# Scores of the first eight attention units: 64 contracted rows against 128 rows with zeros in the queries

## The chip, the cores and the metric

The kernel runs on one core of a Trainium2 chip. The core has five engines with a queue of instructions each: PE (TensorE, matrix products; its weight loads are shown apart as PEld), DVE (VectorE), ACT (ScalarE), POOL (GpSimd) and SP (SyncE, which here only issues DMAs). The metric is the device time of one execution in microseconds (us), lower is better.

## What is computed

Forgetting attention over 4 batches, 8 heads, 576 positions and 64 dimensions, then two MLPs of 512 -> 2048 -> 512 on the 2304 rows, all in float32:

```python
scores = scale * np.matmul(q, k.transpose(0, 1, 3, 2))
cum = np.cumsum(np.maximum(s, 0.0), axis=-1)
bias = -(cum[:, :, :, None] - cum[:, :, None, :])
scores = np.where(causal, -1e9, scores + np.minimum(bias, 0.0))
attn = softmax(scores)            # sum + 1e-09 below
x = matmul(attn, v), heads side by side
x = (s * relu(x @ w_in) ** 2 + b) @ w_out
h = x @ w_in2;  out = (max(h, 0) + alpha * min(h, 0)) @ w_out2
```

## The kernel before

Attention is cut into 32 units: one batch, one pair of heads, and either the first 320 queries (blocks 0, 1, 2) or the last 256 (blocks 3, 4), with all keys up to the last query. A unit's pair of heads lies on the 128 partitions, head 0 on rows 0 to 63 and head 1 on rows 64 to 127.

For each unit `load_qk` brings q and k to a tile `nat`; `transpose_qk` turns both on DVE (L308, in 32x32 blocks) into `turned`, so that the 64 dimensions of each head lie on its half of the partitions; `scores` (L320 on) prepares the bias (DVE L362, POOL L366), multiplies, folds the product into the bias on DVE (L388) and takes the exponential on ACT (L394), and POOL divides by the sum (L403); `values` transposes the probabilities on PE (L434), copies them out of PSUM (L438) and multiplies with v (L450, tile `av`).

Units 0 to 7 are "native": their products are plain float32. For them the scores' product (L384) takes only the head's own half, 64 rows of `turned` as the stationary and 64 as the moving operand. From unit 8 on q and k are split into high and low parts (`xs`, `ql`; L326 to L332), and L386 and L387 multiply on all 128 rows. The eight native units have 48 products at L384; in the trace each is two instructions, so 96 are counted there. Units 1 to 3 are also "early": their buffers are slots of the weight memory that is still empty. Units 4 to 7 hold 256 queries each and 576 keys, the units 0 to 3 320 and 320.

Beside attention runs the first MLP: `load_packet` brings 512 KB pieces of weights, and ACT (L116), DVE (L117, L118), ACT and POOL (L106, L107) turn them into two float32r parts. Row block 0 of the MLP (products L575 and L616) begins when units 0 to 3 are done, and shares the engines with units 4 to 7 and with the conversion of the weights. ACT and DVE form its inner activations (L596, L598, L599), ACT and POOL split them (`gh`, `gl`).

A scheduler orders the instructions of every engine before the launch, by priority in program order and by a timeline of its own; each engine then runs its queue in that fixed order. Tiles with the same tag share memory: a new tile waits for the last reader of the one before it. `turned` has one buffer (tag `turned`) for the units 0 and 4 to 31, so a unit's transposes wait for the last scores product of the unit before. The tiles `ql` are zeroed on the other head's half once, at the start, on POOL (L204).

Of the kernel before, what the change touches and what calls it, by code (L numbers as in the profile page):

```python
# [8 lines left out]
F32 = mybir.dt.float32  # L9
F32R = mybir.dt.float32r  # L10
# [8 lines left out]
def tile_forget_attention__then__two_mlps(  # L19
# [20 lines left out]
    nc = tc.nc  # L40
# [3 lines left out]
    P = 128  # L44
# [7 lines left out]
    R1 = IB[2][1]  # L52
    QK = S - R1 + S
# [12 lines left out]
    one = ctx.enter_context(tc.tile_pool(name="one", bufs=1))  # L66
# [131 lines left out]

    ql_tiles = [[one.tile([P, R1], F32R, tag=f"ql{h}{n}", name=f"ql{h}{n}") for n in range(1 + h)] for h in range(2)]
    for h in range(2):
        for t in ql_tiles[h]:
            nc.gpsimd.memset(t[64 * (1 - h) : 64 * (2 - h)].bitcast(F32), 0.0)  # L204
    vs_tile = one.tile([P, 5 * 4 * D], F32R, tag="vs", name="vs_all")
    nc.gpsimd.memset(vs_tile[0:64, 16 * D :].bitcast(F32), 0.0)

# [3 lines left out]
    HALF = (slice(0, 64), slice(64, 128))  # L211
# [36 lines left out]
    def qk_tiles(u, dtype, tag):  # L248

        nq, nk = u.q1 - u.q0, u.q1  # L250
        if u.early:
            q_tile, k_tile = (u.buf(one, 512, dtype, "", f"{tag}{z}") for z in "qk")
            return [q_tile[:, :nq], k_tile[:, :nk]], q_tile[:, :nq], k_tile[:, :nk]
        both = one.tile([P, QK], dtype, tag=tag, name=f"{tag}_{u.tag}")
        return [both[:, : nq + nk]], both[:, :nq], both[:, nq : nq + nk]

    def load_qk(u):

        u.nats, *parts = qk_tiles(u, F32, "nat")
        for src, dst, t0, t1 in ((q, parts[0], u.q0, u.q1), (k, parts[1], 0, u.q1)):  # L260
            for h in range(2):
                for e in range(2):
                    (nc.scalar if u.n == 0 and src is k else nc.sync).dma_start(  # L263
                        out=dst[64 * h + 32 * e : 64 * h + 32 * (e + 1)].rearrange("p (c d) -> p c d", d=32),
                        in_=src[u.b, u.h0 + h, t0:t1, 32 * e : 32 * (e + 1)].rearrange("(c p) d -> p c d", p=32),
                    )
# [35 lines left out]
    def transpose_qk(u):  # L302


        nq = u.q1 - u.q0
        turned, *u.qk = qk_tiles(u, F32, "turned")
        for dst, src in zip(turned, u.nats):
            nc.vector.transpose(dst, src)  # L308
        yield
        if u.native:  # L310
            return
        if u.n >= 12 and u.n % 2:

            xs = [two.tile([P, 1024], F32R, tag="raw", name=f"xs{h}_{u.tag}") for h in range(2)]
        else:
            xs = [one.tile([P, QK], F32R, tag=f"xs{h}", name=f"xs{h}_{u.tag}") for h in range(2)]
        u.ql = [ql_tiles[h][u.n % len(ql_tiles[h])] for h in range(2)]
        u.xs = [[x[:, :nq], x[:, nq : nq + u.q1]] for x in xs]
        for h in range(2):
            own, other = HALF[h], HALF[1 - h]  # L320
            (qh, kh), (qt, kt) = u.xs[h], u.qk
            if u.early:
                nc.scalar.copy(qh[own], qt[own])
                nc.scalar.copy(kh[own], kt[own])
            else:
                nc.scalar.copy(xs[h][own, : nq + u.q1], turned[0][own])  # L326
            nc.gpsimd.tensor_scalar(
                out=qh[other], in0=qt[own], scalar1=1.0, scalar2=0.0, op0=ALU.mult, op1=ALU.add
            )
            yield  # L330
            nc.vector.tensor_tensor(out=kh[other], in0=kt[own], in1=kh[own].bitcast(F32), op=ALU.subtract)  # L331
            nc.vector.tensor_tensor(  # L332
                out=u.ql[h][own, :nq], in0=qt[own], in1=qh[own].bitcast(F32), op=ALU.subtract
            )
            yield

    def scores(u, h):

        own = HALF[h]
        head = u.b * H + u.h0 + h  # L340
        nr = len(u.blocks)
        nm = two.tile([P, 3], F32, tag="nm", name=f"nm_{u.tag}_{h}")
        sm = two.tile([P, 3], F32, tag="sm", name=f"sm_{u.tag}_{h}")
        if u.rng == 0:
            nc.gpsimd.memset(sm[:, 0:1], 1.0)
        big = None if u.early else two.tile([P, 1088], F32, tag="probs", name=f"probs_{u.tag}_{h}")
        probs, col = {}, 0
        for r in u.blocks:
            i0, i1 = IB[r]
            rows = i1 - i0  # L350
            if u.early and r != 1:
                big, col = u.buf(two, 0, F32, "", f"probs{h}{r}"), 0

            width = -(-i1 // P) * P if i1 < S else S
            pt = probs[r] = big[:, col : col + width]
            col += width
            if width > i1:
                nc.gpsimd.memset(pt[:, i1:], 0.0)  # L358
            if r == 0:
                nc.gpsimd.memset(pt[64:P, 0:64], 0.0)  # L360

            nc.vector.tensor_scalar(  # L362
                out=pt[:rows, :i1], in0=u.cums[h][:rows, :i1], scalar1=cumT[:rows, r, head : head + 1],
                scalar2=0.0, op0=ALU.subtract, op1=ALU.min,
            )
            nc.gpsimd.affine_select(  # L366
                out=pt[:rows, i0:i1], in_=pt[:rows, i0:i1], pattern=[[-1, rows]], base=0,
                channel_multiplier=1, compare_op=ALU.is_ge,
                fill=MASKED,
            )  # L370
        u.probs[h] = probs
        for m, r in enumerate(u.blocks):
            i0, i1 = IB[r]
            rows, n = i1 - i0, i1
            a0 = i0 - u.q0
            pt = probs[r]
            init = KEEP_ALL
            for j0, j1 in ([(0, n)] if n <= 512 else [(0, 320), (320, n)]):
                sc = u.bank("sc", f"sc{h}_{r}_{j0}")

                scr, all_ = sc[:rows, : j1 - j0], sc[:, : j1 - j0]
                aq = slice(a0, a0 + P)
                if u.native:
                    nc.tensor.matmul(all_, u.qk[0][own, aq], u.qk[1][own, j0:j1], start=True, stop=True)  # L384
                else:
                    nc.tensor.matmul(all_, u.xs[h][0][:, aq], u.xs[h][1][:, j0:j1], start=True, stop=False)  # L386
                    nc.tensor.matmul(all_, u.ql[h][:, aq], u.xs[h][1][:, j0:j1], start=False, stop=True)  # L387
                nc.vector.tensor_tensor_reduce(  # L388
                    out=pt[:rows, j0:j1], in0=scr, in1=pt[:rows, j0:j1], scale=-SCALE, scalar=init,
                    op0=ALU.add, op1=ALU.min,  # L390
                    accum_out=nm[:rows, m : m + 1],
                )
                init = nm[:rows, m : m + 1]
            nc.scalar.activation(  # L394
                pt[:rows, :n], pt[:rows, :n], AF.Exp, bias=nm[:rows, m : m + 1], scale=-1.0,
                accum_out=sm[:rows, m : m + 1],
            )
            yield
        nc.vector.tensor_scalar(out=sm[:, :nr], in0=sm[:, :nr], scalar1=1e-9, scalar2=None, op0=ALU.add)
        nc.vector.reciprocal(sm[:, :nr], sm[:, :nr])  # L400
        for m, r in enumerate(u.blocks):
            rows, n = IB[r][1] - IB[r][0], IB[r][1]
            nc.gpsimd.tensor_scalar(  # L403
                out=probs[r][:rows, :n], in0=probs[r][:rows, :n], scalar1=sm[:rows, m : m + 1],
                scalar2=1.0, op0=ALU.mult, op1=ALU.mult,
            )
        yield
# [73 lines left out]
    def attention():  # L481
        nonlocal done
        us = [Unit(n) for n in range(EARLY)]
        load_qk(us[0])
        sum_gates()
        load_cum(us[0])
        load_qk(us[1])
        load_v(us[0])
        load_cum(us[1])
        packet(0, 0)  # L490
        load_qk(us[2])
        load_cum(us[2])
        load_v(us[1])
# [7 lines left out]
        for u in us:  # L501
            split_v(u)
        yield from transpose_qk(us[0])
        yield from alternate(transpose_qk(us[1]), scores(us[0], 0))
        yield from alternate(transpose_qk(us[2]), scores(us[0], 1))
        yield from alternate(transpose_qk(us[3]), scores(us[1], 0), values(us[0], 0))
        yield from alternate(scores(us[1], 1), values(us[0], 1))
        yield from alternate(scores(us[2], 0), values(us[1], 0))
# [226 lines left out]
```

## Time and profile before

| | us |
|---|---|
| median of three runs | 1091.94 (1088.45, 1091.94, 1092.47) |
| the profiled execution | 1088.58 |
| its span, first to last instruction | 1086.8 |
| PE busy | 1045.6 (96%) |
| DVE, ACT, POOL busy | 666.8, 644.4, 478.4 |
| mean granted clock of PE | 0.985 of full speed |

Rows of a table of stretches give: from and to (us from the span's start), length, busy time and number of instructions of each engine, the mean granted clock of PE as a share of full speed (1.00 is 2.4 GHz, 0.50 is 1.2 GHz), the mean busy share of the DMA engines, and GB/s. Rows of a timeline give the start, the time until the end of the last of the instructions put together, engine, line, operation, output and inputs, shape, count, and in brackets the idle time of the engine before them with what ended it. Ends of products are modelled; the distance from one start to the next is the better measure of what a product takes.

### The profile page before, as it was taken

Reading aid. Unit: us, or ns where it says so; the run is one execution under the profiler, and the core shown is the slowest. Engines: PE = TensorE matmul, PEld = TensorE weight load, DVE = VectorE, ACT = ScalarE, POOL = GpSimd, SP = SyncE. Lnnn points to the kernel's source line nnn. Section 1 sums busy time; section 2 is a strip of 40 time slices with the busy share of each in tenths; the row PEclk is TensorE's granted clock in tenths of the full one; section 3 lists DMA queues with packets and bytes.
Section 4 is the critical chain, followed back from the end, with each engine's and each line's share of the span. In section 5 each row is a group of like instructions: output and inputs, shape, how many; then the busy total and the mean of one; then the engine's idle time right before and its main releaser. Section 6 shows DMA issues by size and latency. Waiting matters only on the chain.

```text
span 1086.8 us, 21253 instructions
## 1 busy us (share of the span) xinstructions
PE 1045.6 (96%) x7429; PEld 969.9 (89%) x7429; DVE 666.8 (61%) x1612; ACT 644.4 (59%) x1719; POOL 478.4 (44%) x868
## 2 busy tenths in 40 slices
PE   5899999999999999999999999899999999999998
PEld 3677799999999999999998999789999999999997
DVE  7699878787688877787565167943333333333332
ACT  3686767777767877777565467643444434434332
POOL 6688877665766757666464267820000000000000
PEclk9699899999999999999999999999999999999999
DMA  6987433343232422233134064510100100000000
GB/s 145 236 234 221 136 70 81 80 99 56 50 81 65 109 50 60 67 78 81 34 104 141 12 204 155 175 40 1 40 20 20 40 1 20 2 20 20 2 20 20
DMA packets 170059, 83.85 MB, mean 77 GB/s; under 512 B 135456, under 2 KB 155936, under 8 KB 169952
## 3 DMA queue, kind: packets, MB, share of 16 engines
q1 hardware_dynamic: 168272, 81.94, 28.3%
q8 instruction: 58, 0.95, 0.4%
q10 hardware_dynamic: 1680, 0.57, 0.2%
q14 instruction: 49, 0.40, 0.1%
HBM read 72.96 MB, written 9.51 MB: 76 GB/s over the span
## 4 chain that ended last, share of the span: by engine, by line
PE 67%; DVE 14%; DMA 5%; issue 4%; ACT 4%; POOL 3%; SPq 2%; DVEq 0%; POOLq 0%; ACTq 0%
PE hp L575 29%; PE acc L626 18%; PE acc L616 12%; PE pt L434 3%; DVE probs L362 3%; PE av L450 3%; DMA wo<-in_moe_w_out_dram 2%; DVE probs L388 2%; DVE wt L117 2%; DVE wt L118 2%; SPq L263 1%; DVE r L599 1%; DVE xs L331 1%; PE sc L387 1%; PE sc L386 1%
## 5 line engine op out<-in xcount | busy, mean ns | idle before, releaser
L575 PE MATMUL hp<-xh,w 128*128 128x256 f32 x2304 | 467.5, 285 | 5.6 <-ACT r L596 2.9
L575 PEld LDWEIGHTS hp<-xh,w 128*128 128x128 f32 x2304 | 378.6, 191 | 13.5 <-ACT r L596 4.4
L575 PE MATMUL hp<-xl,w 128*128 128x256 f32 x1152 | 327.2, 284 | 0.0
L575 PEld LDWEIGHTS hp<-xl,w 128*128 128x128 f32 x1152 | 220.3, 191 | 6.3 <-POOL probs L358 0.7
L626 PE MATMUL acc<-w,ring 128*128 128x512 f32 x864 | 220.4, 393 | 1.2 <-POOL ring L107 0.8
L616 PE MATMUL acc<-gh,w 128*128 128x256 f32 x1024 | 201.9, 288 | 5.3 <-ACT gh L106 5.0
L604 DVE SCALAR_TENSOR_TENSOR ring<-ring,nalpha 128x256 f32<-128x256 f32 x144 | 74.6, 520 | 177.3 <-ACT ring L603 176.3
L626 PEld LDWEIGHTS acc<-w,ring 128*128 128x128 f32 x864 | 154.1, 189 | 28.1 <-POOL ring L107 1.2
L616 PEld LDWEIGHTS acc<-gh,w 128*128 128x128 f32 x1024 | 161.1, 191 | 10.7 <-ACT gh L106 7.4
L616 PE MATMUL acc<-gl,w 128*128 128x256 f32 x512 | 149.4, 292 | 2.8 <-POOL gl L107 2.7
L596 ACT ACTIVATE ring<-hp 128x256 f32<-128x256 f32 x144 | 55.5, 385 | 138.6 <-PE hp L575 138.4
L107 POOL TENSOR_TENSOR gl<-r,gh 128x256 fp32r<-128x256 f32 x128 | 99.9, 781 | 63.8 <-ACT gh L106 62.6
L403 POOL TENSOR_SCALAR probs<-probs,sm 64x64 f32<-64x64 f32 (+4 forms) x160 | 93.5, 597 | 61.0 <-DVE sm L400 57.9
L394 ACT ACTIVATE probs<-probs,nm 64x64 f32<-64x64 f32 (+4 forms) x160 | 90.0, 562 | 46.3 <-DVE nm L388 44.9
L599 DVE TENSOR_SCALAR r<-r,gate_s,gate_b 128x256 f32<-128x256 f32 x144 | 80.5, 559 | 58.0 <-ACT r L598 55.8
L106 ACT CAST ring<-ring 128x256 fp32r<-128x256 f32 x144 | 58.5, 407 | 77.3 <-DVE ring L604 65.7
L616 PEld LDWEIGHTS acc<-gl,w 128*128 128x128 f32 x512 | 97.7, 191 | 5.2 <-POOL gl L107 5.1
L107 POOL TENSOR_TENSOR w<-wt,w 128x512 fp32r<-128x512 f32 x63 | 90.4, 1441 | 26.2 <-ACT w L106 22.1
L107 DVE TENSOR_TENSOR ring<-ring,ring 128x256 fp32r<-128x256 f32 x128 | 54.4, 425 | 61.1 <-ACT ring L106 61.1
L434 PE MATMUL pt<-ident,probs 128*128 128x128 f32 x480 | 79.8, 285 | 8.4 <-POOL probs L403 7.8
L388 DVE CUSTOM_DVE_ANT_0 probs<-sc,probs 128x320 f32<-128x320 f32 (+3 forms) x160 | 67.9, 427 | 23.9 <-PE sc L387 18.4
L596 ACT ACTIVATE r<-hp 128x256 f32<-128x256 f32 x144 | 54.6, 379 | 39.3 <-PE hp L575 33.2
(86 smaller groups left out, 1637.2 us busy)
## 6 DMA issues: line engine op xcount, KB each, us to landing
wi<-in_moe_w_in_dram SPq DMA_DIRECT2D x32, 512.0 KB, 4.5
wo<-in_moe_w_out_dram SPq DMA_DIRECT2D x32, 512.0 KB, 5.0
cum<-cum_d SPq DMA_DIRECT2D x32, 288.0 KB, 3.5
cum<-cum_d SPq DMA_DIRECT2D x30, 160.0 KB, 3.1
nat<-in_k_dram SPq DMA_DIRECT2D x64, 72.0 KB, 2.3
x_d<-res SPq DMA_DIRECT2D x18, 256.0 KB, 2.4
x<-x_d SPq DMA_DIRECT2D x9, 512.0 KB, 4.3
out_dram<-res SPq DMA_DIRECT2D x18, 256.0 KB, 2.0
```

Of the source, the lines that this page charges most:

```text
L106: nc.scalar.copy(hi, src)
L107: lo_eng.tensor_tensor(out=lo, in0=src, in1=hi.bitcast(F32), op=ALU.subtract)
L388: nc.vector.tensor_tensor_reduce(out=pt[:rows, j0:j1], in0=scr, in1=pt[:rows, j0:j1], scale=-SCALE, scalar=init, op0=ALU.add, op1=ALU.min, ...
L394: nc.scalar.activation(pt[:rows, :n], pt[:rows, :n], AF.Exp, bias=nm[:rows, m : m + 1], scale=-1.0, accum_out=sm[:rows, m : m + 1],)
L403: nc.gpsimd.tensor_scalar(out=probs[r][:rows, :n], in0=probs[r][:rows, :n], scalar1=sm[:rows, m : m + 1], scalar2=1.0, op0=ALU.mult, op1=A ...
L434: nc.tensor.transpose(tp[:, o : o + P], u.probs[h][r][:, k0 : k0 + P], ident)
L575: nc.tensor.matmul(hs, a[:, c], b[:, c], start=(n == 0), stop=(n == len(terms) * NCC - 1))
L596: nc.scalar.activation(r, hs, AF.Relu, scale=1.0 / W_SCALE)
L599: nc.vector.tensor_scalar(out=r, in0=r, scalar1=gate_s[:, 0:1], scalar2=gate_b[:, 0:1], op0=ALU.mult, op1=ALU.add)
L604: nc.vector.scalar_tensor_tensor(out=r, in0=u, scalar=nalpha[:, f : f + 1], in1=r, op0=ALU.mult, op1=ALU.add)
L616: nc.tensor.matmul(acc[:, d], a[:, d * P : (d + 1) * P], b, start=(f == 0 and d % 2 == 0 and n == 0), stop=(f == NF - 1), skip_group_check ...
L626: nc.tensor.matmul(accs[:, m * DM : (m + 1) * DM], a[:, m * P : (m + 1) * P], b, start=(f == 0 and b is woh and a is gh), stop=(f == NF - ...
```

## The change

The queries of the native units go into one of three pairs of zeroed tiles, `qz`, taken in turn (unit number modulo 3). Tile h of a pair holds the queries of head h on its own half and zeros on the other half, so that the product over all 128 rows of queries and keys is the score of that one head. The keys of both heads stay together in one tile.

- The pairs lie in memory that is unused until unit 8: two in the tags `xs0` and `xs1`, the third in the tags `ql00` and `ql10`. The first pair is zeroed on DVE, the other two on POOL, at the start.
- The three tiles `ql` are now made and zeroed (POOL) in the first call of `transpose_qk` for a unit that isn't native, unit 8.
- For a native unit DVE makes three transposes in place of one (unit 0, units 4 to 7) or two (units 1 to 3): the keys on 128 partitions, then the queries of each head on 64 partitions.
- L384 multiplies `qz[h]` with the keys on all 128 rows.
- The early units take one slot of weight memory less each.

```diff
-    ql_tiles = [[one.tile([P, R1], F32R, tag=f"ql{h}{n}", name=f"ql{h}{n}") for n in range(1 + h)] for h in range(2)]
-    for h in range(2):
-        for t in ql_tiles[h]:
-            nc.gpsimd.memset(t[64 * (1 - h) : 64 * (2 - h)].bitcast(F32), 0.0)
+    def zeroed(h, tile_, eng):
+        eng.memset(tile_[64 * (1 - h) : 64 * (2 - h)].bitcast(F32), 0.0)
+        return tile_
+
+    qz = []
+    for n in range(3):
+        if n < 2:
+            both = one.tile([P, QK], F32, tag=f"xs{n}", name=f"qz{n}")
+            pair = [both[:, :R1], both[:, R1 : 2 * R1]]
+        else:
+            pair = [one.tile([P, R1], F32, tag=f"ql{h}0", name=f"qz{n}{h}") for h in range(2)]
+        qz.append([zeroed(h, t, nc.gpsimd if n else nc.vector) for h, t in enumerate(pair)])
+    ql_tiles = []
...
         u.nats, *parts = qk_tiles(u, F32, "nat")
+        u.nat = parts
...
         nq = u.q1 - u.q0
+        if u.native:
+            kt = u.buf(one, 512 if u.early else QK, F32, "turned", "turnedk")[:, : u.q1]
+            nc.vector.transpose(kt, u.nat[1])
+            u.qk = [q_[:, :nq] for q_ in qz[u.n % 3]], kt
+            for h in range(2):
+                nc.vector.transpose(u.qk[0][h][HALF[h]], u.nat[0][HALF[h]])
+            yield
+            return
         turned, *u.qk = qk_tiles(u, F32, "turned")
         for dst, src in zip(turned, u.nats):
             nc.vector.transpose(dst, src)
         yield
-        if u.native:
-            return
+        if not ql_tiles:
+            for h in range(2):
+                tiles = [one.tile([P, R1], F32R, tag=f"ql{h}{n}", name=f"ql{h}{n}") for n in range(1 + h)]
+                ql_tiles.append([zeroed(h, t, nc.gpsimd) for t in tiles])
...
-                    nc.tensor.matmul(all_, u.qk[0][own, aq], u.qk[1][own, j0:j1], start=True, stop=True)
+                    nc.tensor.matmul(all_, u.qk[0][h][:, aq], u.qk[1][:, j0:j1], start=True, stop=True)
```

## Rows read from the trace of the kernel before

**Rows 1.** The page, span in 40 slices: granted clock of PE in tenths.
```profile
PEclk9699899999999999999999999999999999999999
```

**Rows 2.** Stretches: PE, PEld, DVE, ACT, POOL busy (count), PEclk, DMA share, GB/s.
```profile
28.00:47.00 19.00, 18.60 (x64) 12.49 (x62) 9.48 (x45) 12.24 (x39) 10.25 (x26) 0.55 0.86 206
57.00:85.00 28.00, 27.82 (x166) 22.42 (x164) 26.41 (x51) 21.23 (x50) 23.51 (x26) 0.94 0.90 255
85.00:111.00 26.00, 21.88 (x126) 17.77 (x124) 25.40 (x48) 18.32 (x42) 21.22 (x23) 0.93 0.77 215
111.00:134.00 23.00, 22.80 (x126) 18.81 (x127) 20.41 (x37) 16.61 (x41) 20.09 (x23) 0.85 0.49 134
165.00:560.00 395.00, 388.19 (x3181) 381.69 (x3180) 306.00 (x842) 289.00 (x776) 257.84 (x539) 1.00 0.31 70
```

**Rows 3.** Stretches at half clock; the last row: PE and PEld of L384 alone.
```profile
30.00:47.00 17.00, 16.60 (x52) 11.26 (x51) 8.61 (x41) 11.21 (x34) 8.53 (x20) 0.50 0.86 212
88.00:91.30 3.30, 3.30 (x16) 3.19 (x16) 3.30 (x6) 2.11 (x6) 1.72 (x3) 0.50 0.46 81
112.00:118.50 6.50, 6.50 (x25) 5.21 (x25) 6.50 (x15) 5.01 (x13) 4.58 (x6) 0.50 0.51 117
...
30.00:47.00 17.00, 5.93 (x16) 2.85 (x15) 0.50 0.86 212
```

**Rows 4.** Timeline of PE around three runs of products.
```profile
36.89 2.07 PE L384 MATMUL sc<-turnedk,turnedq 64*128 64x192 f32 x6
38.90 0.69 PE L434 MATMUL pt<-ident,probs 128*128 128x128 f32 x2
...
75.32 1.95 PE L450 MATMUL av<-pf,vn 128*128 128x256 f32 x10
77.08 0.36 PE L575 MATMUL hp<-xh,w 128*128 128x256 f32 x1
...
80.02 0.27 PE L434 MATMUL pt<-ident,probs 128*128 128x128 f32 x1
80.22 1.23 PE L384 MATMUL sc<-turned 64*128 64x320 f32 x4
81.39 0.51 PE L616 MATMUL acc<-gh,w 128*128 128x256 f32 x2
81.73 1.04 PE L434 MATMUL pt<-ident,probs 128*128 128x128 f32 x8
82.53 0.36 PE L575 MATMUL hp<-xh,w 128*128 128x256 f32 x1
```

**Rows 5.** Timeline of PE: the longest idle times before instructions, 85 to 145 us.
```profile
87.11 1.07 PE L384 MATMUL sc<-turned 64*128 64x448 f32 x2 [0.68 <-DVE turned L308]
111.19 0.51 PE L616 MATMUL acc<-gh,w 128*128 128x256 f32 x2 [1.88 <-ACT gh L106]
141.48 0.33 PE L434 MATMUL pt<-ident,probs 128*128 128x128 f32 x1 [0.43 <-POOL probs L403]
```

**Rows 6.** Chain that ended last, in order of time: start, us, what.
```profile
31.11 0.45 PE pt L434
...
36.96 0.95 PE sc L384 x3
...
38.31 0.66 SPq L263
```

**Rows 7.** The transposes: all of L308 (ns min/median/max, first and last start), and timeline of DVE.
```profile
L308 DVE STREAM_TRANSPOSE turned<-nat x29: 823/1023/1037, 6.0 to 509.3; 128x832 f32<-128x832 f32 x16, 128x640 f32<-128x640 f32 x13
L308 DVE STREAM_TRANSPOSE turnedq<-natq x3: 471/492/497, 11.0 to 26.0; 128x320 f32<-128x320 f32 x3
...
86.02 1.03 DVE L308 STREAM_TRANSPOSE turned<-nat 128x832 f32<-128x832 f32 x1
86.98 0.44 DVE L388 CUSTOM_DVE_ANT_0 probs<-sc,probs,nm 128x256 f32<-128x256 f32 x1
```

**Rows 8.** The zeroing of the tiles ql, all of L204.
```profile
L204 POOL MEMSET ql<- x3: 358/358/364, 1.0 to 1.7; 64x320 f32 x3
```

## The prediction

> **What bounds the kernel now.** I read the slices first, then tables of stretches, then PE's timeline where the change lies. The slices show where the clock of PE falls: only in the first 135 us [rows 1]. The stretches show who is full. From 165 us on PE is busy 388 of 395 us at full clock [rows 2]; the later stages are alike, so what is won or lost before that point reaches the end one for one, and nothing behind it touches the change. All of L384 lies before 134 us. There three stages differ. From 28 to 47 us PE is busy 18.6 of 19 us while DVE, ACT and POOL are about half idle, and PE's clock is 0.55 [rows 2]: PE at half speed (1.2 GHz) is the bound, with DMA (0.86) close behind. From 85 to 111 us DVE is busy 25.4 of 26 us and PE 21.9 [rows 2]: DVE, full of weight conversions, is the bound. From 57 to 85 us both are nearly full. From 111 to 134 us PE is busy 22.8 of 23 us, DVE 20.4: PE again, part of it at half clock [rows 2, 3].
>
> **Part A, 64 rows become 128.** The products keep their columns. What goes is what surrounds them. The run of v products takes 1.76 us from its start to the next start, for 256, 256, 256, 192 and 64 columns: 1.72 ns a column [rows 4]. A burst of scores of 320 + 256 columns would take 0.99 us at that rate; it takes 1.17 (80.22 to 81.39), and the one transpose record before it takes 0.20 from start to start where eight take 0.80, or 0.10 each [rows 4]. So 0.18 + 0.10 = 0.28 us a burst belong to the passage into and out of 64 rows. Units 4 to 7 have four bursts each; 13 start between 57 and 134 us. Four start after 111 us (111.7, 121.9, 125.7, 131.8), where PE has no gap: 4 x 0.28 = 1.1 us, counted in full. The other nine (2.5 us) lie where DVE is full or nearly so and PE already waits for it, as at 87.11 [rows 2, 5]: I count 0 of them (bounds 0 and 2.5).
>
> **Part B, the clock.** PE fell to half clock at about 30, 57, 88 and 112 us, each time after it had stood idle; the idle time of 1.88 us at 111.19 is one [rows 2, 3, 5]. What differs is how long it stayed low. From 57 us, with one burst of scores at the start, it was back after 3.4 us (0.94 of 28 us), and from 88 us, with a single record of 64-row scores left, after 3.4 too. From 112 us, with a burst of scores behind the fall, it stayed 6.9 us, and from 30 us, where 5.9 of 16.6 busy us are 64-row scores, 17 us, though PE was never long idle [rows 3]. No row shows what 128-row scores would do; the ends are no change and no fall at all. I take the length of the rows with few scores, 3.4 us, for all.
> From 112 us this brings back 3.4 us at half clock, worth 1.7 us, on a stretch that PE bounds (bounds 0 and 3.4).
> From 30 us, the chain of waits tells how much of the time passes on: it goes through PE from 31.11 to 37.91 us and then to the loads on SP at 38.31 [rows 6]. With full clock from 33.4 us, the 4.5 us of PE work left to 37.91 take half: 2.2 us. Ends: only the passages of two bursts, 0.6, and all 6.8 us at full clock, 3.4. DMA is busy 0.86 of 19 us [rows 2], so more than 2.7 us could not pass on without a better use of DMA, which is why I don't go beyond the middle.
>
> **Part C, the transposes on DVE.** Units 4 to 7 had one of 832 columns, 1.03 us, 0.96 from start to start; one of 320 takes 0.49 [rows 7]. Between them a column costs about 1.05 ns, so 576 columns take 0.76 and 256 take 0.43: three make 1.62, and with 0.07 of overlap at each of two more joints the queue grows by 0.45 us. If half the partitions cost half (no row shows a 64-partition transpose), it would be 0.02; without overlap 0.59. I take 0.45, since shapes that differ in columns alone are the nearest rows. The transposes of units 5, 6 and 7 fall into the full stretch (86.02 is one): 3 x 0.45 = 1.4 us on DVE's path (bounds 0.1 and 1.8). For units 0 to 4 the gain of 0.4 to 0.5 us each is covered by DVE's idle half before 47 us; without that cover, 2.2 us more. Against that, the queries go to three pairs in turn and need not wait for the scores of the unit before; only the keys do (0.76 instead of 1.03). I count nothing for it.
>
> **Part D, zeroing.** At the start two memsets go to DVE and one more than before to POOL, some 0.36 us each [rows 8], well before the first transposes at 6.0 us [rows 7]: nothing. The three of `ql` move to unit 8, about 134 us, in POOL's queue ahead of the casts for `xs` and the divisions for PE's transposes: 3 x 0.36 = 1.1 us. PE waits for POOL there once, 0.43 us at 141.48 [rows 5]; I take 0.4 (bounds 0 and 1.1). The waits of unit 8's `xs` for `qz` end no later than its own transposes, which wait for the same scores. One slot less for each early unit shifts which weights wait for which buffer; those weights are converted long after the early units: nothing.
>
> **Sum**, against the profiled execution of 1088.58: -1.1 (A) - 1.7 - 2.2 (B) + 1.4 (C) + 0.4 (D) = -3.2, so 1085.4. The runs stand at two levels, 1088.45 and 1088.58 against 1091.94 and 1092.47, 3.5 us apart, which is what 7 us of half clock would cost. The median shown is of the upper level. After the change the lower should be the commoner one; I add 0.6 for the other: **1086.0**.
>
> **Rivals.**
> *DVE takes it all.* PE is spared, but DVE hands out the work: up to 111 us the gain of B turns into waits like that of 87.11, and what PE saves after 111 turns into waits for `gh`. For it: DVE full over 85 to 111 us. Against it: PE without a gap from 111 to 134 us. Time: 1088.58 + 1.4 + 0.4 = 1090.4. That the passages and the clock don't depend on the rows at all, so that the change doesn't do what it says, gives the same.
> *More comes through.* B at its upper ends (3.4 + 3.4), the nine bursts too (2.5), A (1.1), C and D at their lower ends: -10.3, 1078.3. For it: DVE is half idle before 47 us and could convert earlier; against it: DMA at 0.86 to 0.90.
> *Three transposes in a row before each first score.* If the planned queue of DVE puts the queries behind the keys, after the last score of the unit before, PE waits 0.45 us more for `turned` in each of units 1 to 7, 3.2 us; with C at 1.4 and D at 1.1 and no gain that makes +5.7: 1094.3, slower. For it: PE does wait for `turned` (0.68 at 87.11). Against it: before 47 us DVE has room, and the queries may run early. It decides once these waits are over about 0.9 us each.
> *Two heads beside each other.* The row of scores from 36.89 to 38.90 has six records of 192, 320 and 64 columns, 576 in 2.01 us; at half clock and the v products' rate that is 1.98 [rows 4]: nothing ran beside anything. If bursts of two heads did overlap, full rows would lose about half of each of 13 bursts, +6.5, 1095.1. The Trainium skill (TensorEngine Tiling (Array Packing), Performance Considerations) recommends two row tiles where 64 rows are contracted, and under Tiling Modes it says that different tiles run in parallel; by it this change goes the wrong way. This trace shows no such gain, so its chance is 0.01.
>
> **How the numbers follow.** The forecast gets 0.45 (0.28 of it faster by over 0.5%, below 1086.5; 0.17 within), DVE takes it all 0.25 (0.22 within, 0.03 slower), more comes through 0.17 (faster), three in a row 0.12 (0.09 slower, if the upper level comes on top and makes 1097.8; 0.03 within), two heads 0.01 (slower). 0.5% is about what a measurement of this kernel can tell from no change. So faster 0.45, same 0.42, slower 0.13. The range goes from the lower edge of more comes through, 1078.5, to 1095.5, past three in a row.
>
> **What would show it.** After the change bursts of 576 columns should take 1.0 us from start to start at full clock, and a transpose record before them 0.10. The half clock from 30 us should end by 34 us, and no low stretch should hold for 6.9 us. DVE should show 0.76 and 0.43 us for the new transposes, and PE's idle time for `turned` should not grow. Low clock unchanged from 30 to 47 us would strike out B; idle time of PE between 57 and 134 us grown by some 3 us would mean that DVE took it. A shift of more than 5 us behind 165 us would mean that the scheduler's order, not these parts, made the difference.

## Result and the profile after

| | before | after |
|---|---|---|
| median of eight runs each, us | 1090.97 (1088.45 to 1092.99) | 1097.74 (1094.27 to 1098.1) |
| ratio, 95% interval | | 1.0056 (1.0043 to 1.007) |
| the profiled execution, us | 1088.58 | 1097.69 |

The change makes the kernel slower by 0.56%, 6 us. The forecast was 1086.0; the time lies above the upper end of the range, 1095.5. The two profiled executions are 9.1 us apart, since that of before lies low among its runs; comparisons of traces below carry those 2 us too much.

The page of after: busy time of the engines, PE's granted clock by slices. Then the stretches of [rows 2], and the rest of the span, first for before, then for after.

```profile
PE 1035.4 (94%) x7429; PEld 969.9 (89%) x7429; DVE 681.4 (62%) x1627; ACT 645.6 (59%) x1719; POOL 482.2 (44%) x872
PEclk9899899999999999999999999999999999999999
```

```profile
28.00:47.00 19.00, 15.78 (x74) 12.21 (x75) 15.90 (x53) 13.45 (x43) 10.69 (x28) 0.83 0.85 207
57.00:85.00 28.00, 24.19 (x153) 20.54 (x152) 26.38 (x53) 21.33 (x50) 22.65 (x26) 0.98 0.80 243
85.00:111.00 26.00, 22.08 (x148) 19.18 (x148) 25.73 (x45) 18.45 (x43) 24.98 (x27) 1.00 0.81 235
111.00:134.00 23.00, 19.10 (x107) 16.11 (x106) 21.75 (x39) 15.47 (x37) 18.37 (x21) 0.85 0.47 129
165.00:560.00 395.00, 383.35 (x3130) 376.94 (x3129) 313.65 (x847) 288.19 (x775) 257.99 (x541) 1.00 0.31 71
```

```profile
560.00:1086.80 526.80, 513.30 (x3460) 472.68 (x3459) 225.72 (x431) 247.57 (x660) 94.65 (x91) 1.00 0.16 53
```

```profile
560.00:1095.90 535.90, 522.55 (x3534) 482.72 (x3532) 225.89 (x438) 252.48 (x672) 97.86 (x96) 1.00 0.16 52
```

PE is busy 10 us less (1035.4 against 1045.6) in a span that is 9 us longer. From 28 to 47 us its clock is 0.83 where it was 0.55 [rows 2]. But at 560 us it has 74 instructions more to go than before, 9 us at 0.12 us each, and that difference stays to the end. Of the 74, 51 are lost between 165 and 560 us, where the change touches nothing: PE does 3130 instructions there against 3181 [rows 2]. If the start of the same product (`hp`) is compared in both traces, after is 3.0 us behind at 166 us and 9.4 at 567. Not all of these 6.4 us are a loss of after: the execution of before that was profiled was a quick one. The same change in the order of before (first experiment below) falls back against it too, from 2.4 us ahead at 166 us to 1.0 behind at 567. Against that kernel, which computes the same, after is 5.4 us behind at 166 us and 8.4 at 567: so about half of its loss or more lies before 165 us.

Now the change itself, in PE's and DVE's timelines and the groups of transposes and memsets.

```profile
58.68 0.27 PE L455 MATMUL pt<-ident,probs 128*128 128x128 f32 x1
58.79 1.14 PE L405 MATMUL sc<-turnedk,qz 128*128 128x320 f32 x4
59.76 1.19 PE L471 MATMUL av<-pf,vn 128*128 128x320 f32 x6
```

```profile
L319 DVE STREAM_TRANSPOSE turnedk<-nat x5: 481/768/772, 6.1 to 113.0; 128x576 f32<-128x576 f32 x4, 128x320 f32<-128x320 f32 x1
L322 DVE STREAM_TRANSPOSE qz<-nat x10: 427/442/507, 5.4 to 96.3; 64x256 f32<-64x256 f32 x8, 64x320 f32<-64x320 f32 x2
L322 DVE STREAM_TRANSPOSE qz<-natq x6: 471/506/510, 7.1 to 27.2; 64x320 f32<-64x320 f32 x6
...
L203 POOL MEMSET ql<- x3: 355/357/526, 8.0 to 85.7; 64x320 f32 x3
```

A burst of 576 columns takes 0.97 us from start to start and the transpose record before it 0.11, where they took 1.17 and 0.20 [rows 4]: the passage is gone here. (At 70.06 us it is the same; at the other four bursts of this size other records follow, and the values are 0.79 to 1.24 and 0.16 to 0.17.) The new transposes take 0.77 and 0.44 us; one of 320 columns takes 0.51 us on 64 partitions and took 0.49 on 128 [rows 7], so 64 partitions cost what 128 do. The zeroing of `ql` is over by 86 us, long before unit 8 needs it.

Part of what is lost shows in PE's waits from 165 to 620 us: what waited, for what, total us, times, the longest. First before, then after, then the kernel of the second experiment, which computes what before does in the order of after.

```profile
PE hp L575 <- ACT r L596: 2.5, 5, 0.8
PE acc L616 <- ACT gh L106: 2.1, 4, 0.7
PE acc L616 <- POOL gl L107: 1.6, 3, 0.7
PE pt L434 <- POOL probs L403: 1.1, 3, 0.7
PE av L450 <- DVE pl L107: 0.9, 3, 0.5
```

```profile
PE pt L455 <- POOL probs L424: 3.2, 3, 2.5
PE hp L596 <- ACT r L617: 3.1, 5, 1.4
PE av L471 <- DVE pl L107: 2.6, 6, 1.2
PE acc L637 <- ACT res L658: 1.8, 1, 1.8
```

```profile
PE pt L434 <- POOL probs L403: 3.4, 4, 2.6
PE hp L575 <- ACT r L596: 2.7, 3, 1.7
PE av L450 <- DVE pl L107: 2.6, 6, 1.2
PE acc L616 <- ACT res L637: 1.7, 1, 1.7
```

From 165 to 620 us PE waits 14.6 us in after (rows left out included) and 8.2 in before. The longest wait of before is 0.8 us; after has one of 2.5 and one of 1.8. The third block repeats the second nearly wait by wait, though its computation is that of before: these waits come with the order of the instructions. The whole change in the order of before waits 10.9 us there, never more than 0.8 at once.

Before 165 us (from 24 us on) the longest wait of after is one for ACT's copy `pf`, 5.3 us before 54.20. The kernel of the second experiment has it too; in before all waits for `pf` are 0.2 us. After, then the second experiment:

```profile
PE av L471 <- ACT pf L459: 9.5, 6, 5.3
...
PE av L450 <- ACT pf L438: 4.2, 1, 4.2
```

### The profile page after: what moved, and what is told of

It is laid out like the page before. It is cut to its first block, busy times and chain, and to the rows that moved or that the text cites. A ratio compares the mean times of both kernels' runs of the same rounds, so it can differ in the third digit from the quotient of the medians.

```text
span 1095.9 us, 21276 instructions
## 1 busy us (share of the span) xinstructions
PE 1035.4 (94%) x7429; PEld 969.9 (89%) x7429; DVE 681.4 (62%) x1627; ACT 645.6 (59%) x1719; POOL 482.2 (44%) x872
## 4 chain that ended last, share of the span: by engine, by line
PE 67%; DVE 14%; issue 5%; DMA 5%; ACT 4%; POOL 3%; SPq 2%; DVEq 0%; POOLq 0%; ACTq 0%
PE hp L596 29%; PE acc L647 18%; PE acc L637 12%; PE av L471 3%; PE pt L455 3%; DVE probs L383 2%; DVE wt L117 2%; DVE probs L409 1%; SPq L274 1%; DVE wt L118 1%; DVE xs L352 1%; DVE r L620 1%; PE sc L408 1%; DMA wo<-in_moe_w_out_dram 1%; PE sc L407 1%
## 5 line engine op out<-in xcount | busy, mean ns | idle before, releaser
L424 POOL TENSOR_SCALAR probs<-probs,sm 64x64 f32<-64x64 f32 (+4 forms) x160 | 96.8, 617 | 63.7 <-DVE sm L421 59.9
L455 PE MATMUL pt<-ident,probs 128*128 128x128 f32 x480 | 79.7, 283 | 12.6 <-POOL probs L424 11.6
```

The costliest lines, as they stand in the source:

```text
L424: nc.gpsimd.tensor_scalar(out=probs[r][:rows, :n], in0=probs[r][:rows, :n], scalar1=sm[:rows, m : m + 1], scalar2=1.0, op0=ALU.mult, op1=A ...
L455: nc.tensor.transpose(tp[:, o : o + P], u.probs[h][r][:, k0 : k0 + P], ident)
```

## Experiments

The scheduler orders anew whenever the program changes. Of PE's 7319 instructions in the built programs, before and after have 5621 in common order. Two explanations stood against each other: the order makes the difference, or the change's own costs do. So I separated the two: a kernel in a held order gives each instruction of an engine an ordering edge (no wait on the chip) to the one that precedes it in a recorded order. New instructions stand where those stood that they replace.

```python
for a, b in zip(row, row[1:]):      # row: one engine's instructions as recorded
    tc.add_manual_dep(b, a.name, ...)   # order only
```

"Old order" is that of before, "new order" that of after. In the traces PE's 7429 records stand, one for one, in the sequence in which a kernel was held. "Before" and "after" themselves are the free kernels.

**The change in the old order.**

> The whole change, with the queues of all engines held in the order of the kernel before: the three transposes stand where the one stood, the zeroing of ql just ahead of unit 8's first cast on POOL. Theory 1 (the new order lost the time): faster than before by 0 to 4 us, so 8 us or so faster than the changed kernel. Theory 2 (the three transposes on a full DVE lost it): slower than before by 4 to 7 us, like the changed kernel.

Measured: 0.9996 (0.9979 to 1.0012). With the queues as they stood, the change makes no difference that can be measured; Theory 2's 4 us are excluded. The 0.56% come with the order.

**The computation of before in the new order.**

> The computation of the kernel before (64 rows, one transpose a unit), with the queues of all engines held in the order that the scheduler gave to the changed kernel. Theory 1 (order): slower than before by 6 to 12 us, since it has the new order without what the 128 rows bring. Theory 2 (transposes): within 2 us of before.

Measured: 1.0065 (1.0042 to 1.0088). The order alone costs as much as the whole change or a little more.

**128 rows alone**, in the old order: every other cost of the change left out.

```diff
-nc.tensor.matmul(all_, u.qk[0][own, aq], u.qk[1][own, j0:j1], start=True, stop=True)
+nc.tensor.matmul(all_, u.qk[0][:, aq], u.qk[1][:, j0:j1], start=True, stop=True)
```

> The kernel before with one edit: L384 multiplies all 128 rows of turned, so a score is the sum over both heads (left out: the separation of the heads; no zeros, no further transposes, no further memsets). The order of every engine's queue is held as in the kernel before. So only the rows of the products differ. Theory 1 (the passages into and out of 64 rows and the half clock cost PE time, and the loss of the change came from the new order of the queues): faster than before by 2 to 6 us, the low clock from 30 us ends by about 34 to 37 us, bursts of 576 columns take 1.0 us in place of 1.17. Theory 2 (DVE is the bound and takes whatever PE saves): within 1.5 us of before, with PE's idle time between 30 and 134 us grown by what its products became shorter.

Measured: 0.9979 (0.9963 to 0.9995). A gain of 2.3 us (0.5 to 4.0), where parts A and B had 5.0: at the lower edge of Theory 1, and Theory 2's 1.5 us are not excluded. The stretch from 24 to 165 us of before, then stretches of this kernel:

```profile
24.00:165.00 141.00, 129.48 (x746) 105.72 (x744) 118.42 (x282) 98.17 (x256) 110.64 (x171) 0.89 0.67 176
```

```profile
24.00:165.00 141.00, 120.89 (x760) 104.66 (x761) 124.92 (x293) 100.32 (x263) 113.03 (x177) 0.94 0.67 178
...
28.00:47.00 19.00, 14.96 (x76) 11.90 (x76) 16.17 (x53) 15.53 (x49) 13.58 (x31) 0.84 0.80 199
...
57.00:134.00 77.00, 68.50 (x432) 59.52 (x431) 72.36 (x133) 55.46 (x131) 65.36 (x73) 0.95 0.72 206
...
85.00:111.00 26.00, 21.77 (x126) 18.31 (x126) 25.38 (x46) 18.43 (x42) 21.50 (x23) 0.90 0.80 228
```

PE's waits in that kernel, 24 to 165 us:

```profile
PE pt L434 <- POOL probs L403: 8.6, 7, 2.5
PE acc L616 <- ACT gh L106: 4.4, 5, 2.2
PE acc L616 <- POOL gl L107: 2.4, 3, 1.2
```

PE's busy time falls by 8.6 us, and only 14 more instructions get done. The time in which PE does nothing grows from 11.5 to 20.1 us, as Theory 2 had it: PE now waits 8.6 us for POOL's `probs`, where it waited 5.8, and for `gh` and `gl`. The gain arises where the prediction had it, before 60 us (64 instructions become 76 from 28 to 47 us; the same product starts 2.6 us earlier at 60). From 85 to 111 us DVE is full as before, 126 instructions are done as before, and at 166 us 1.7 us are left. The two profiled executions end together, at 1086.8 and 1086.7 us: they show where the gain arises, and the 2.3 us come from the runs.

**64 rows with the rest of the change**, in both orders, and **128 rows alone in the new order**.

```diff
-nc.tensor.matmul(all_, u.qk[0][h][:, aq], u.qk[1][:, j0:j1], start=True, stop=True)
+nc.tensor.matmul(all_, u.qk[0][h][own, aq], u.qk[1][own, j0:j1], start=True, stop=True)
```

> The changed kernel with one edit: its scores' products take only the head's own 64 rows of qz and of the keys, as before. Order of the queues as in the changed kernel. Theory 1: slower than the changed kernel by 2 to 6 us (about 8 to 12 slower than before), with half clock from about 27 us lasting 10 us or more. Theory 2: within 1.5 us of the changed kernel.

> The changed kernel with the head's own 64 rows in the products, in the order of before: what is left of the change are the three transposes, the zeroing and the buffers. Together with rows128_old_order and after_old_order it closes the square. If the parts add: 1 to 3 us slower than before. If the transposes cost nothing and 128 rows gave nothing in the whole change: within 1 us.

> All 128 rows of turned in L384, so a score is the sum over both heads (left out: the separation of the heads), one transpose a unit, in the order that the scheduler gave to the changed kernel; beside before_new_order only the rows differ. If 128 rows give PE's time back in this order too: 2 to 4 us faster than before_new_order, so 3 to 6 us slower than before. If the waits of this order take it: within 1.5 us of before_new_order, 6 to 8 us slower than before.

Their results are in the table below. In the new order 64 rows are 1.2 us slower than the changed kernel. That lies in Theory 2's 1.5 us and misses Theory 1's 2 to 6, though an uncertainty of some 4 us excludes neither, and the trace has no half clock before 51.2 us, where 10 us of it from about 27 us were expected. In the old order +3.8 us is over the 1 to 3 expected if the parts add. 128 rows alone in the new order are 3.9 us faster than 64 rows there, as the first case had it.

With these three all eight combinations stand side by side (ratio, and us against before):

| | old order | new order |
|---|---|---|
| 64 rows, one transpose (before) | 1, 0 | 1.0065 (1.0042 to 1.0088), +7.1 |
| 128 rows, one transpose | 0.9979 (0.9963 to 0.9995), -2.3 | 1.0029 (1.0009 to 1.0049), +3.2 |
| 64 rows, three transposes, zeroing | 1.0035 (1.0022 to 1.0048), +3.8 | 1.0067 (1.0037 to 1.0097), +7.3 |
| 128 rows, three transposes, zeroing | 0.9996 (0.9979 to 1.0012), -0.4 | 1.0056 (1.0043 to 1.007), +6.1 |

128 rows give -2.3, -4.2, -3.9 and -1.2 us, mean -2.9. Three transposes and the zeroing cost +3.8, +1.9, +0.2 and +2.9, mean +2.2. The new order costs +7.1, +5.5, +3.5 and +6.5, mean +5.7. Each of these differences is uncertain by 2 to 4 us, so the smaller ones can't be told from nothing; the signs agree.

**Which half of the order costs.** The computation of before, with the new order up to 165 us and the old one behind, and the reverse.

> The computation of the kernel before. What its queues hold in the first 165 us stands in the order that the scheduler gave to the changed kernel, all behind it in the order of before. The new order all the way cost 7 us against before. Theory 1a (the loss comes from the new order around the changed units and the weight conversion, before 165 us): 5 to 7 us slower than before. Theory 1b (most of it comes from the order of units 9 to 31, which the change doesn't touch): 1 to 3 us slower; the trace of the new order stood 3 us behind at 165 us.

> The computation of the kernel before, the counterpart: the order of before for what the queues hold in the first 168 us, then the new order. Theory 1a: within 1.5 us of before. Theory 1b: 4 to 6 us slower.

Measured: 1.0033 (1.0017 to 1.0049) and 1.0019 (1.0003 to 1.0036). That is 3.6 and 2.1 us. Both halves cost; together 0.52% of the 0.65%. Neither "only the early stage" nor "only what follows" holds.

**Only units 0 to 3 changed**, in the old order; units 4 to 7, where DVE is full, keep one transpose and 64 rows.

```diff
-        if u.native:
+        if u.n < EARLY:
...
+        if u.native:
+            return
...
-                if u.native:
+                if u.native and u.n >= EARLY:
+                    nc.tensor.matmul(all_, u.qk[0][own, aq], u.qk[1][own, j0:j1], start=True, stop=True)
+                elif u.native:
```

> The change for the units 0 to 3 alone, units 4 to 7 as before, the order of the queues as before. In the same order 128 rows alone gained 2.3 us and the whole change nothing, so transposes and zeroing cost about 2 us. If DVE's full stretch from 57 us on is where the transposes cost, this keeps the gain of the early stretch and sheds the cost: 1 to 3 us faster than before. If the transposes cost among the early units, or the gain of 128 rows lies in the units 4 to 7: within 1 us of before.

Measured: 1.0001 (0.9983 to 1.0018). The first case, 1 to 3 us faster, did not come: leaving out the units in the full stretch of DVE brings nothing over the whole change. Which of the two reasons of the second case holds is not shown.

**Other edits that make the scheduler order anew.** In the computation of before, either the zeroing of `ql` moves to unit 8, or one memset of 0.3 us moves from POOL to DVE (the edit shown):

```diff
-    nc.gpsimd.memset(vs_tile[0:64, 16 * D :].bitcast(F32), 0.0)
+    nc.vector.memset(vs_tile[0:64, 16 * D :].bitcast(F32), 0.0)
```

> The kernel before with one edit: the three tiles ql are zeroed for unit 8 and not at the start (three memsets of POOL, 1.1 us, moved). The scheduler orders the queues anew, and the order that it finds shares no more with before than that of the changed kernel does (5615 of 7319 instructions of PE in common sequence, against 5621). If such a new order costs by itself: 3 to 10 us slower. If the order of the changed kernel was slow for what the change did to it: within 2 us of before.

> The kernel before with one memset of 0.3 us (the zeros of vs_all at the start) on DVE in place of POOL; nothing else. The scheduler then finds the same order for PE as for ql_late, which was 0.66% slower than before. If the order alone costs: 5 to 9 us slower than before. If ql_late was slow because its memsets stood in POOL's way at unit 8: within 1.5 us of before.

Measured: 1.0066 (1.0041 to 1.009) and 1.0066 (1.005 to 1.0083). Both edits give PE one and the same order, a third one, with 5615 instructions in common order with before. An edit of 0.3 us costs 7 us, as much as the change under study. The kernel with the moved memset is 4.8 us ahead of before at 225 us and 7.3 behind at 468, so it loses more than the changed one in the units that no edit touches, 3118 instructions of PE against 3181 [rows 2]:

```profile
165.00:560.00 395.00, 379.80 (x3118) 374.64 (x3117) 313.36 (x849) 287.93 (x775) 261.83 (x538) 1.00 0.31 72
```

**The whole change, ordered freely, with a plan close to the old one.** With every pair of `qz` and that memset on DVE, the scheduler returns to the old order after about an eighth of PE's instructions.

```diff
-        qz.append([zeroed(h, t, nc.gpsimd if n else nc.vector) for h, t in enumerate(pair)])
+        qz.append([zeroed(h, t, nc.vector) for h, t in enumerate(pair)])
-    nc.gpsimd.memset(vs_tile[0:64, 16 * D :].bitcast(F32), 0.0)
+    nc.vector.memset(vs_tile[0:64, 16 * D :].bitcast(F32), 0.0)
```

> The whole change; only the zeroing at the start is done otherwise: all of qz and the zeros of vs_all on DVE (five memsets of about 0.36 us before 3 us, where DVE waits for the gates). The scheduler orders it freely, and with this it falls back into the order of before: from the second eighth of PE's instructions on the sequence is the same. If the order is what cost the 6 us: within 2.5 us of before and 4 to 8 us faster than the changed kernel. If the three transposes or the full rows cost them: 4 to 8 us slower than before.

Measured: 0.9988 (0.9973 to 1.0003). The same change, without any held order, is back at the time of before and 7 us below the changed kernel. It does not beat before by what can be measured.

## One of the new waits, followed back

The wait of 2.54 us at 215 us, in the timelines of PE, DVE and POOL of after:

```profile
215.43 0.90 PE L455 MATMUL pt<-ident,probs 128*128 128x128 f32 x3 [2.54 <-POOL probs L424]
...
208.92 1.29 DVE L352 TENSOR_TENSOR xs<-turned,xs 64x576 fp32r<-64x576 f32 x1
210.22 0.59 DVE L353 TENSOR_TENSOR ql<-turned,xs 64x256 fp32r<-64x256 f32 x1
...
213.46 0.75 DVE L352 TENSOR_TENSOR xs<-turned,xs 64x576 fp32r<-64x576 f32 x1 [0.34 <-ACT xs L347]
...
209.67 0.86 POOL L107 TENSOR_TENSOR vs_all<-vn,vs_all 64x128 fp32r<-64x128 f32 x1
...
213.62 2.53 POOL L424 TENSOR_SCALAR probs<-probs,sm 64x64 f32<-64x64 f32 x3
```

The same work in before:

```profile
207.96 0.55 PE L434 MATMUL pt<-ident,probs 128*128 128x128 f32 x3 [0.75 <-POOL probs L403]
...
203.09 0.75 DVE L331 TENSOR_TENSOR xs<-turned,xs 64x576 fp32r<-64x576 f32 x1
203.85 0.42 DVE L332 TENSOR_TENSOR ql<-turned,xs 64x256 fp32r<-64x256 f32 x1
...
207.73 1.29 DVE L331 TENSOR_TENSOR xs<-turned,xs 64x576 fp32r<-64x576 f32 x1 [1.09 <-ACT xs L326]
...
205.19 0.46 POOL L107 TENSOR_TENSOR vs_all<-vn,vs_all 64x128 fp32r<-64x128 f32 x1 [1.99 <-ACT vs_all L106]
...
207.19 1.22 POOL L403 TENSOR_SCALAR probs<-probs,sm 64x64 f32<-64x64 f32 x3
```

From the start of `xs` to the transpose on PE it takes 4.87 us in before and 6.51 in after: 1.64 of the 1.79 us by which the wait is longer. The instructions are the same, with other neighbours. In before POOL's `vs_all` comes after DVE's `xs` and `ql`; in after they lie beside each other, and all three are slower (0.86 for 0.46; 1.29 for 0.75; 0.59 for 0.42). Then come POOL's three divisions and DVE's next `xs`: in before the divisions start first, take 1.22 us, and DVE's `xs` takes 1.29; in after `xs` starts first, takes 0.75, and the divisions, for which PE waits, take 2.53. The kernel with the computation of before in the new order has this wait too, 2.55 us at 215.59, and so have 128 rows alone in the new order (2.54 at 210.69) and the kernel that has the new order only behind 168 us (2.55 at 210.90). Of the kernels with the old order at this place, which number seven, 64 rows with three transposes has it as well (2.49 at 211.20) and the one with the new order up to 165 us has 1.63; the others have 0.9 or less. So the wait is in every trace of the new order, but it can come in the old one too.

At the end of this wait PE falls to half clock in after, for 3.4 us, where before has full clock from 119 to 1084 us:

```profile
215.20:218.60 3.40, 3.17 (x15) 3.18 (x16) 2.23 (x7) 0.97 (x3) 1.76 (x4) 0.50 0.55 90
```

At half the rate that is up to 1.7 us more (an estimate). The fall does not come each time: with the same wait, 128 rows alone in the new order keep full clock there.

This explains one wait. It is not shown to be the cause of the whole: summed over DVE's instructions from 165 to 620 us, the time above the shortest instance of each operation and shape (of all traces) is 71.6 us in before and 74.9 in after. But it is 71.1 in the kernel of before in the new order, which is as slow as after, and 75.8 in the change in the old order, which is as fast as before. Slowed instructions are everywhere; what seems to differ is whether PE waits behind them. Which reordered pairs make up the other 4 us stays open.

## Why the prediction was wrong

**The step that failed** is in the first paragraph: "so what is won or lost before that point reaches the end one for one, and nothing behind it touches the change". It takes the order of the queues as given. Every term of the sum is reckoned for queues in the order of before, and the new order that the scheduler makes of the changed program stands in it at nothing, without a reason. The runs show what it costs: 7.1 us with the computation of before, 5.7 on the mean of four pairs, more than any term. The last part of the prediction named a sign of it, a shift of more than 5 us behind 165 us, but gave it no price, no rival and no chance. That the sign came is in part luck: the 6.4 us are measured against a quick execution of before, against the change in the old order it is 3.0 (8.4 less 5.4), and about half of the loss or more lies ahead of 165 us, where the sign doesn't look.

**Part A** was right as a mechanism (0.97 for 1.17, 0.11 for 0.20). **Part B** shows its direction in the old order only. By the mean granted clock of all runs (rounded so that it tells the time to about 1 us), the time at half clock (1.2 GHz) has there a median of 21.8 us in before and 27.3 with 64 rows and three transposes, but 15.2 in both kernels with 128 rows. The trace of the change in the old order has three stretches of 3.4 us, from 32.4, 52.8 and 83.6 us, and none at 112, about as forecast. In the new order the medians are 24.1 with 64 rows and 19.7 with 128 where there is one transpose, and 20.9 and 27.4 where there are three: the changed kernel as it ran was not less at half clock than before. Its trace has half clock from 27.5 us for 6.8 us, and again for 6.8 from 51.4 and 112.8; and with the computation of before in the new order PE keeps full clock until 53.2 us although its products have 64 rows. So the rows alone don't decide whether the clock is low there.

Together A and B, -5.0 in the sum, measure -2.9 (-2.3 in the old order). The term was mis-sized because the time that PE saves from 28 to 47 and from 111 to 134 us does not pass on in full. The rival "DVE takes it all" describes part of the rest: PE's idle time from 57 to 134 us, which was to grow by some 3 us, goes from 4.5 us [rows 2] to 8.5 with 128 rows alone and to 11.6 in after. But what PE then waits for directly is POOL's divisions (8.6 us) and the parts of `gh` (6.8) more than DVE.

**Parts C and D**, +1.8 together, measure +2.2 on the mean, with single values from 0.2 to 3.8. C rests on 0.45 us a unit, and the change in the old order shows a little more, 1.59 us from the first start to the next instruction for three transposes:

```profile
82.83 0.77 DVE L319 STREAM_TRANSPOSE turnedk<-nat 128x576 f32<-128x576 f32 x1
83.52 0.87 DVE L322 STREAM_TRANSPOSE qz<-nat 64x256 f32<-64x256 f32 x2
84.42 0.48 DVE L409 CUSTOM_DVE_ANT_0 probs<-sc,probs,nm 128x256 f32<-128x256 f32 x1
```

against 0.96 [rows 7]; +0.63. D's 0.4 was wrong in place: the memsets ran by 86 us, off the path. What the late `ql` does cost comes through the plan, +7 us in the run that has it alone.

**Three transposes in a row** gave +5.7 us, near the measured 6, but by luck; the reason was another: PE's waits for the keys before 165 us are 2.9 us in after and 1.0 in before, but the new order without the three transposes has 2.7 (one wait) too, and the change in the old order shows 0.7 for `qz` as its largest wait for a transpose.

**The forecast for the change in the old order**, for which the sum was made, is -3.2 us against the execution of 1088.58; measured are -0.4 (-2.3 to +1.3). That lies between the forecast and "DVE takes it all" (+1.8), and neither fits. The times themselves, 1086.0 and 1090.4, mislead beside a median of runs, since 1088.58 was a quick execution. The two levels for which the prediction added 0.6 us don't show either: 75 later runs of before fill the range from 1086.9 to 1097.3 us.

## What to carry to other kernels

Where a scheduler replans the whole program, an edit's time is the edit plus a new plan; here the plan was worth up to 7 us, and the two sides of the edit -2.9 and +2.2 us on the mean. Before crediting or blaming an edit, run it in the order of the old kernel, or run an edit that does nothing, to see how much the plan alone moves. A saving on one engine in a stretch where a second is full turns into waiting: price the stretch by what the other engines hand out, and count the gain only up to there. And compare traces of kernels that differ in one thing: an execution that happens to be quick looks like an effect.

## What was not expected of the hardware

A VectorE instruction that reads two operands stood for as long as GpSimd's queue ran beside it. DVE's `xs` takes 0.75 us by itself and 3.45 here, until POOL's run that begins at 328.64 (three divisions, `gl`, a short memset, `vs_all`) ends at 331.57:

```profile
328.73 3.45 DVE L352 TENSOR_TENSOR xs<-turned,xs 64x576 fp32r<-64x576 f32 x1 [0.36 <-ACT xs L347]
...
328.64 1.21 POOL L424 TENSOR_SCALAR probs<-probs,sm 64x64 f32<-64x64 f32 x3
329.82 0.74 POOL L107 TENSOR_TENSOR gl<-r,gh 128x256 fp32r<-128x256 f32 x1
...
330.56 1.01 POOL L107 TENSOR_TENSOR vs_all<-vn,vs_all 128x384 fp32r<-128x384 f32 x1
```

The trace of before has the same case at 321.06, 3.44 us. The Trainium skill (SBUF — State Buffer, SBUF: two separate sides) says that the two engines share a pair of ports which one holds for a whole instruction while the other stands; these rows agree, and here `xs` stood through the whole run of POOL's instructions and not through one.

The spread of the runs of before goes with the clock: over 75 runs the time at half clock, by the mean granted clock, lies between 10.9 and 43.8 us, and a run is longer by 0.20 us for each (correlation 0.70; that the clock is the cause is not shown). By that slope a fifth of the time at half clock reached the end, where part B counted half of it from 112 us.
